# Fused attention and two MoE layers on one core: transfers weighed by issue and latency, squares of r after reload, a third staging buffer, and 42 identity matmuls among the first heads

## The chip, the cores and the metric

One NeuronCore of a Trainium2 chip runs the whole program. The metric is the device time of one execution in microseconds. The matrix engine is PE (TensorE), the others are DVE (VectorE), ACT (ScalarE), POOL (GpSimd) and SP (SyncE), which issues the DMA transfers. PE's granted clock has two levels, 1.2 and 2.4 GHz; the profile gives it as a share of the upper one.

## The reference

```python
# q, k, v: (4, 8, 576, 64); causal window of 128, ALiBi
scores = np.where(mask, q @ k.T / 8 + bias, -1e9)     # mask: 0 <= i - j < 128
x  = softmax(scores) @ v                              # heads merged: 2304 x 512
y  = (((x @ w1) * (x @ w2)) @ w3) @ w_out             # 512 -> 1024 -> 1024 -> 512
h  = np.maximum(y @ w_in, 0.0)                        # 512 -> 2048
out = (h * h) @ w_out2                                # 2048 -> 512
```

All of it is float32 (`moe_w1`, `moe_w2`, `moe_w3`, `moe_w_out`, `moe2_w_in`, `moe2_w_out` stand here as w1, w2, w3, w_out, w_in, w_out2).

## The kernel before, in words

**Arithmetic.** Most products are made from two rounded words per operand, a high and a low one, in three matmuls: high x high, high x low, low x high (`mm3`, L165 to 168). So each operand is prepared by a cast to the high word and a subtraction that gives the low word; the cast may run on ACT (`act_copy`, L171) or DVE (L221), the subtraction on DVE or POOL (L174). Native float32 matmuls take two passes of PE each instead.

**Stages.** Four follow each other, and overlap through the planner's order.
- *Heads.* 32 heads: scores of K and Q (L463 to 466), softmax on DVE, ACT and POOL, transposes by identity (L486 to 498), and probabilities times V. The heads in the set NQ have native scores, those in NV native PV (L520, L542, L543); the others use split words (L525 to 529, L549). Beside the heads, w3 @ w_out is folded into one matrix, w34, with native matmuls (L730), up to 126 us.
- *ab and y*, 126 to 526 us, among the remaining heads: x @ w1, x @ w2 and y = (a*b) @ w34, in groups of 12 matmuls of 288 columns that accumulate in a PSUM tile with the tag g. The pool ps_g has three banks of it (L156). DVE, as it takes the product out of PSUM, makes `gf` (L783), then `gt`'s words. y goes to DRAM (`y_scr`).
- *r*, 526 to 710: relu(y @ w_in) squared, with Strassen-Winograd: seven products P1 to P7 for each of 3 blocks j of 768 tokens and 8 blocks m of weights. The sums of products (L1089) are made on DVE into C; ACT does relu (L1115) and square (L1116) in place, and C is stored to DRAM (`s_scr`).
- *out*, 713 to 893: the squares times w_out2, 9 blocks t of 256 tokens, again seven products (X<-u,st and X<-u,ww, 128x256). `add_o` loads four blocks of s_scr (tags fo and fq, 128x1024), forms the sums (L1160), casts and subtracts them into operand words (tags st for t = 0 and ww).

**Words of w_in and w_out2.** They come as raw pairs of words (`w2io`), are merged by DVE and ACT (`m_load` L902, scale L215 or L294, L304, `m_last` L913) and stored to DRAM as `m_scr` (`m_store`, L919): the *merges*, 385 to 485 us. Later `add_words2` loads them back into a staging buffer, makes the Strassen combinations, and splits these into the tags u and v6. y is loaded back for j = 0, 1, 2 by `add_yops` into yA and yB. The staging buffers are st (two) and s0 (one); s0 holds the words of i0, i1 and o7.

**Order.** The order of instructions comes from `Plan` (L27): every piece of work is a task with a rank, a cost per engine it may run on, the tasks that it depends on, and the buffers that it takes and gives back. `run` keeps a model time per engine (pe, a, d, p, dma), puts the task that could start earliest next (within LOOK, the lowest rank), and picks the engine by its end plus `bias`. A result on another engine counts as ready a latency later (L253). All tasks are emitted in that order, and each engine runs its own in that order: a wait of one instruction holds all behind it on its engine. `w_dma` (L243) is the model cost of a transfer on SP's queue. `p_warm` (L616) is four 128x256 matmuls of `bm` ahead of all other work of PE.

```python
# L156 and L616
    ps_g = ps1.enter_context(tc.tile_pool(name="ps_g", bufs=3, space=PSUM))
    def p_warm():
        t = ps_t.tile([128, 512], F32, tag="t", name="t")
        for _ in range(4):
            nc.tensor.matmul(t[:, 0:256], ident, bm, start=True, stop=True)
```

Of the kernel before, what the change touches and what calls it, by code (L numbers as in the profile page):

```python
# [8 lines left out]
F32 = mybir.dt.float32  # L9
# [7 lines left out]
NV = frozenset(range(7))  # L17
RANK = dict(w34=6.25, h0=-10.7, w12=37.2, w12s=7.96, w12l=9.7)
# [9 lines left out]
class Plan:  # L28
# [9 lines left out]
    bias = dict(d=3.0, D=0.34, a=0.3, p=0.0)  # L38
# [14 lines left out]
    def run(self):  # L53
# [71 lines left out]
def fused_kernel(  # L125
# [117 lines left out]
    def w_dma(kb):  # L243
        return 0.1 + kb / 300.0
# [8 lines left out]
        dict(pe=0.25, a=0.2, d=0.12, p=0.2, dma=2.0, gate=0.0),  # L253
# [362 lines left out]
    def p_warm():  # L616
        t = ps_t.tile([128, 512], F32, tag="t", name="t")
        for _ in range(4):
            nc.tensor.matmul(t[:, 0:256], ident, bm, start=True, stop=True)

    hold("warm", "t", 1)
    add("warm", -100.0, {"pe": 5.0}, lambda e: p_warm(), [], ["warm"], ["warm"])
# [4 lines left out]
    def add_head(n, rank):  # L627
# [12 lines left out]
        if nq:  # L640
            add(f"ldq{n}", r, {"dma": w_dma(295)}, lambda e: t_load_qk(n), [f"ldq{n - 1}"] if n else [], H_("qk"))
            add(f"kn{n}", r, w_ts(576, "Dap"), lambda e: t_kn(n, e), N("ldq"))
            qd = N("kn")
        else:
            hold(f"qkraw{n}", "qkraw", 4)
            add(f"ldq{n}", r, {"dma": w_dma(590)}, lambda e: t_load_qk(n), [f"ldq{n - 1}"] if n else [], [f"qkraw{n}"])
# [6 lines left out]
        if nv:  # L653
            add(f"ldv{n}", r + 0.1, {"dma": w_dma(147)}, lambda e: t_load_v(n), N("ldq"), H_("vs"))
            vd = N("ldv")
        else:
            hold(f"vraw{n}", f"vraw{n % 2}", 2)
            add(f"ldv{n}", r + 0.1, {"dma": w_dma(147)}, lambda e: t_load_v(n), N("ldq"), [f"vraw{n}"])
# [291 lines left out]
    def add_words2(k, m, rank, stag, dep=()):  # L950
# [12 lines left out]
        for part, w, tag in (("a", 1024, "u"), ("b", 768, "u" if m < 2 else "v6")):  # L963
            hold(f"w{part}{z}", tag, n * (4 if part == "a" else 3))

# [11 lines left out]
            add(f"wh{part}{z}", rank + 0.1, w_copy(w), hi, d, [f"w{part}{z}"], g_)  # L977
# [16 lines left out]
    def add_yops(j, rank, deps):  # L994
        where = ["yA"] * 14 if j != 1 else ["yB"] * 6 + ["yA"] * 8
        for c in range(2):
            z = f"{j}{c}"
            tag, t2 = ("u", "t2a") if j == 0 else ("st", ("t2a", "t2b")[c])
# [6 lines left out]
                deps + [f"sy{b}{hf}{c + 2 * k}" for b, hf in ys_ for k in range(2)], ["ym" + z])  # L1005
# [17 lines left out]
            for pos, P in enumerate(PO):  # L1023
# [12 lines left out]
                add(f"yo0{j}{P}{c}", rank + pos, w_copy(TN), hi, [get[1] + z], [f"yo{j}{P}{c}"], g_)  # L1036
# [30 lines left out]
    def add_group(g, n, order, prod, fin, rank):  # L1067
# [17 lines left out]
        add("c1" + z, -20, w_copy(n, True), lambda e: copy(e, t_("c1", "c1"), bank[g, 1]), ["P1" + z], ["c1" + z], [f"X1{z}"])  # L1085
# [16 lines left out]
    def add_r(j, m, rank, last):  # L1102
# [8 lines left out]
        def fin(z):  # L1111
            def sq(e, c):
                x = cs[g, c]
                if e == "a":
                    nc.scalar.activation(out=x, in_=x, func=ACTF.Relu)  # L1115
                    nc.scalar.activation(out=x, in_=x, func=ACTF.Square)  # L1116
                else:
                    ENG[e].scalar_tensor_tensor(out=x, in0=x, scalar=0.0, in1=x, op0=ALU.max, op1=ALU.mult)
# [5 lines left out]
            for c in ("11", "12", "21", "22"):  # L1124
                add(f"sq{c}{z}", rank + 16, {"a": 2 * w_copy(TN)["a"]}, lambda e, c=c: sq(e, c), [f"c{c}{z}"])
# [10 lines left out]
    def add_o(t, rank, last):  # L1136
        j, t0 = divmod(256 * t, 2 * TN)
        ft = {k: ("fo" if t == 0 and k[0] == "A" else v) for k, v in FT.items()}
        for k, n in (("A11", 4), ("A12", 3), ("A21", 4), ("A22", 3), ("S1", 3), ("S2", 5)):
            hold(f"f{k}{t}", ft[k], n)  # L1140
        for k in ("A11", "A21", "A22", "A12"):
# [8 lines left out]
            col = (t0 + 128 * i) // TN  # L1150
            add(f"lf{k}{t}", rank - 20, {"dma": w_dma(524)}, ld,
# [23 lines left out]
        for pos, P in enumerate(order):  # L1175
# [63 lines left out]
    add("q2", 0, {"gate": 0.0}, lambda e: open_q2(), last_r + [f"wlao{NM - 1}", f"wlbo{NM - 1}"])  # L1239
# [18 lines left out]
    add_yops(2, 2000 + 112 - 14, done(1))  # L1258
# [62 lines left out]
```

## Time and profile before

| | us |
|---|---|
| median of 3 runs | 900.42 (900.16 to 902.66) |
| the profiled execution | 901.4 |
| its span | 899.6 |
| PE busy in the span | 871.2 |
| DVE, ACT, POOL busy | 696.4, 502.4, 205.6 |
| mean granted clock of PE | 0.992 of full |

The span goes from the first to the last instruction; the execution's own time has a little around it. A row of a timeline gives the start, how long it was from there to the end, the engine, the line, the operation with what it writes and reads, the tile, the count of instructions that it stands for, and in brackets the idle time of the engine before it with what ended it. Matmuls are pipelined: the distance from one start to the next is what each costs, and the duration of one is longer. A line of waits gives the total, the number and the longest.

### The profile page before, as it was taken

The page shows a single profiled execution, that of the slowest core. Times are in us where ns is not written, and L with a number is a line of the kernel's source. Part 1 is how long each engine was busy: PE and PEld are TensorE (multiplying, and loading weights), DVE is VectorE, ACT ScalarE, POOL GpSimd, SP SyncE. Part 2 cuts the span into 40 slices and gives each one's busy share as a digit, 9 for nine tenths or more (in the row PEclk, how much of TensorE's full clock was granted, in tenths as well). Part 3 has the DMA queues.
Part 4 walks back from the last instruction along what each step waited for, and adds up shares of the span by engine and source line. Part 5 has one row for each costly group of instructions (what it writes and reads, how often), then busy time and mean ns, then how long its engine had stood idle before and what let it go on. Part 6 is the DMA issues. An engine that isn't in the chain of part 4 may idle for free.

```text
span 899.6 us, 16224 instructions
## 1 busy us (share of the span) xinstructions
PE 871.2 (97%) x5888; PEld 805.3 (90%) x5888; DVE 696.4 (77%) x1402; ACT 502.4 (56%) x1086; POOL 205.6 (23%) x252
## 2 busy tenths in 40 slices
PE   7999999999999899999999999989999799999998
PEld 4544479999999899999989999989999799999998
DVE  5777888788877888878666938776568888998882
ACT  5777775656566567676323336776677733222220
POOL 4423422213231232311000134542136400000000
PEclk8999999999999999999999999999999899999999
DMA  7786312433426425163667034643385475445310
GB/s 239 270 296 201 127 48 80 133 74 81 134 49 186 114 72 157 35 186 101 233 233 237 25 109 153 204 165 116 113 255 176 144 210 165 118 136 152 101 54 30
DMA packets 90704, 128.43 MB, mean 143 GB/s; under 512 B 8832, under 2 KB 70784, under 8 KB 88576
## 3 DMA queue, kind: packets, MB, share of 16 engines
q1 hardware_dynamic: 90624, 127.40, 45.6%
q8 instruction: 46, 0.75, 0.3%
q14 instruction: 34, 0.28, 0.1%
HBM read 90.67 MB, written 36.70 MB: 142 GB/s over the span
## 4 chain that ended last, share of the span: by engine, by line
PE 80%; DMA 9%; DVE 7%; ACT 2%; issue 2%; SPq 1%; POOL 0%; DVEq 0%; ACTq 0%; POOLq 0%
PE X L168 13%; PE X L167 13%; PE X L166 13%; PE g L166 7%; PE g L168 7%; PE g L167 7%; PE g L730 7%; DMA u<-in_w2io_dram 3%; DMA m_scro<-u 2%; PE s L463 2%; PE a L520 2%; PE s L466 1%; PE t L486 1%; PE s L465 1%; DMA m_scri<-u 1%
## 5 line engine op out<-in xcount | busy, mean ns | idle before, releaser
L166 PE MATMUL g<-x,wu 128*128 128x288 f32 x512 | 154.2, 301 | 3.1 <-DVE gf L783 2.0
L168 PE MATMUL g<-x,wu 128*128 128x288 f32 x512 | 151.1, 295 | 1.7 <-DVE wu L174 1.7
L167 PE MATMUL g<-x,wu 128*128 128x288 f32 x512 | 151.6, 296 | 0.1
L166 PEld LDWEIGHTS g<-x,wu 128*128 128x128 f32 x512 | 96.3, 188 | 4.9 <-DVE gf L783 3.7
L168 PEld LDWEIGHTS g<-x,wu 128*128 128x128 f32 x512 | 96.5, 188 | 1.9 <-DVE wu L174 1.9
L167 PEld LDWEIGHTS g<-x,wu 128*128 128x128 f32 x512 | 96.8, 189 | 0.3 <-DVE x L174 0.3
L166 PE MATMUL g<-gt,wu 128*128 128x288 f32 x256 | 76.6, 299 | 0.2 <-DVE gt L221 0.2
L167 PE MATMUL g<-gt,wu 128*128 128x288 f32 x256 | 75.8, 296 | 0.1
L168 PE MATMUL g<-gt,wu 128*128 128x288 f32 x256 | 75.5, 295 | 0.0
L1089 DVE TENSOR_TENSOR C<-X,U 128x384 f32<-128x384 f32 (+1 forms) x99 | 51.0, 518 | 24.4 <-PE X L168 11.1
L443 ACT ACTIVATE e<-e,st 128x256 f32<-128x256 f32 (+1 forms) x128 | 60.5, 475 | 14.0 <-DVE st L435 13.6
L1115 ACT ACTIVATE C<-C 128x384 f32<-128x384 f32 x96 | 49.5, 515 | 32.6 <-DVE C L1089 32.5
L168 PE MATMUL X<-yA,u 128*128 128x384 f32 x192 | 65.2, 340 | 1.6 <-DVE u L174 1.6
L167 PE MATMUL X<-yA,u 128*128 128x384 f32 x192 | 65.0, 339 | 0.0
L166 PE MATMUL X<-yA,u 128*128 128x384 f32 x192 | 65.0, 339 | 0.0
L938 POOL TENSOR_TENSOR st<-st 128x256 f32<-128x256 f32 (+1 forms) x52 | 46.7, 916 | 76.4 <-DMA st<-m_scri 37.1
L730 PE MATMUL g<-raw 128*128 128x512 f32 x128 | 63.2, 625 | 0.0
L213 POOL TENSOR_SCALAR e<-e,st 128x256 f32<-128x256 f32 (+1 forms) x61 | 31.0, 520 | 122.1 <-DVE st L453 73.0
L167 PE MATMUL X<-u,ww 128*128 128x256 f32 x198 | 55.4, 280 | 0.0
L168 PE MATMUL X<-u,ww 128*128 128x256 f32 x198 | 55.4, 280 | 0.0
L166 PE MATMUL X<-u,ww 128*128 128x256 f32 x198 | 55.4, 280 | 0.0
L171 ACT ACTIVATE pt<-t 128x512 fp32r<-128x512 f32 (+1 forms) x64 | 38.2, 597 | 28.0 <-PE t L498 18.5
(218 smaller groups left out, 2651.4 us busy)
## 6 DMA issues: line engine op xcount, KB each, us to landing
s_scr<-C SPq DMA_DIRECT2D x96, 192.0 KB, 1.9
u<-in_w2io_dram SPq DMA_DIRECT2D x32, 512.0 KB, 4.4
qkraw<-in_qk_dram SPq DMA_DIRECT2D x46, 288.0 KB, 4.3
fo<-s_scr SPq DMA_DIRECT2D x20, 512.0 KB, 4.5
raw<-in_w3t_dram SPq DMA_DIRECT2D x8, 1024.0 KB, 6.1
raw<-in_w_dram SPq DMA_DIRECT2D x8, 1024.0 KB, 5.1
fq<-s_scr SPq DMA_DIRECT2D x16, 512.0 KB, 4.6
y_scr<-ye SPq DMA_DIRECT2D x32, 144.0 KB, 3.1
```

What stands on the lines that cost most here:

```text
L166: nc.tensor.matmul(o, wh, xh, start=start, stop=False)
L167: nc.tensor.matmul(o, wh, xl, start=False, stop=False)
L168: nc.tensor.matmul(o, wl, xh, start=False, stop=stop)
L171: nc.scalar.activation(out=o, in_=i, func=ACTF.Copy)
L213: nc.gpsimd.tensor_scalar(out=o, in0=i, scalar1=c, scalar2=1.0, op0=ALU.mult, op1=ALU.mult)
L443: nc.scalar.activation(out=e, in_=e, func=ACTF.Exp, bias=st[:, 0, i:i + 1], scale=-1.0, accum_out=st[:, 1, i:i + 1],)
L463: nc.tensor.matmul(o, qb, d["kh"][:, k0:k1], start=True, stop=True)
L520: nc.tensor.matmul(a[:, 128 * kb:128 * kb + w], vs[:, kb, :], pt[:, 0, c:c + w], start=kb == 0, stop=kb == 2,)
L730: nc.tensor.matmul(gw[fi], wl, wr, start=c == 0, stop=c == 7)
L938: ENG[e].tensor_tensor(out=o, in0=a, in1=b, op=op)
L1089: nc.vector.tensor_tensor(out=t_(o, tag), in0=bank[g, P], in1=cs[g, i], op=ALU.add)
L1115: nc.scalar.activation(out=x, in_=x, func=ACTF.Relu)
```

## The change

1. *Model of transfers.* `w_dma` counts 0.55 us per DMA issue, or kb/300 if that is more, in place of 0.1 + kb/300; a transfer's latency is 3.0, was 2.0. Some ranks and DVE's bias are other numbers. The model only sets the order: with these numbers the merges begin earlier, and the last DVE sequences in which a merge is locked between groups' evacuations are three, where before they were about five.
2. *Fills.* `p_warm` goes. 42 matmuls of the identity with itself (128x128, native) are tasks of very high rank that the planner places where PE would otherwise be idle for over 0.15 us of model time. All of them write one tile of the tag g, which is given back after the last.
3. *NV* holds nine heads, not seven.
4. *Squares.* In r, `fin` only takes the relu; the square is made on ACT after the reload in `add_o` (tasks fs, 128x1024), and what used the loaded block now uses its square.
5. *Third staging buffer.* s0 also takes the words of i2, o2 and o5 and the first half of y for j = 1 and 2, whose load for j = 1 waits only for the third words of i and no longer for the eighth; o7 goes to st.
6. *High words* of the weights, of y for j > 0, of out's operands, and the copy c1 are cast on ACT alone (`w_act`), no longer on DVE.
7. *Border.* The last group of r takes its products in the order 1, 7, 2, 4, 6, 5, 3; the operands of P1 and P2 of t = 0 have a rank lower by 30; the pool q2 opens after the words of o5, not o7.

PE's matmuls go from 5742 to 5770, DVE's instructions from 1404 to 1383, ACT's from 928 to 895, POOL's from 257 to 239; SP issues 426 in both.

```diff
-NV = frozenset(range(7))
-RANK = dict(w34=6.25, h0=-10.7, w12=37.2, w12s=7.96, w12l=9.7)
+FILL = 9000
+NFILL = 42
+NV = frozenset(range(9))
+RANK = dict(w34=5.49, h0=-13.66, w12=35.93, w12s=7.96, w12l=7.68)
-    bias = dict(d=3.0, D=0.34, a=0.3, p=0.0)
+    bias = dict(d=2.02, D=0.34, a=0.3, p=0.0)
-                t0 = 0.0
+                t0 = free.get("pe", 0.0) + 0.15 if rank >= FILL else 0.0
+    def w_act(n):
+        return {"a": 0.2 + n * 0.00094}
-    def w_dma(kb):
-        return 0.1 + kb / 300.0
+    def w_dma(kb, n=1):
+        return max(0.55 * n, kb / 300.0)
-        dict(pe=0.25, a=0.2, d=0.12, p=0.2, dma=2.0, gate=0.0),
+        dict(pe=0.25, a=0.2, d=0.12, p=0.2, dma=3.0, gate=0.0),
-    hold("warm", "t", 1)
-    add("warm", -100.0, {"pe": 5.0}, lambda e: p_warm(), [], ["warm"], ["warm"])
+    fills = [None]
+
+    def p_fill(i):
+        if i == 0:
+            fills[0] = ps_g.tile([128, 512], F32, tag="g", name="g")
+        nc.tensor.matmul(fills[0][:, 0:128], ident, ident, start=True, stop=True)
+
+    NF = NFILL
+    hold("fill", "g", NF)
+    for i in range(NF):
+        add(f"fill{i}", FILL + i, {"pe": 0.22}, lambda e, i=i: p_fill(i), [f"fill{i - 1}"] if i else [],
+            [] if i else ["fill"], ["fill"])
...
-            add(f"wh{part}{z}", rank + 0.1, w_copy(w), hi, d, [f"w{part}{z}"], g_)
+            add(f"wh{part}{z}", rank + 0.1, w_act(w), hi, d + room, [f"w{part}{z}"], g_)
-            tag, t2 = ("u", "t2a") if j == 0 else ("st", ("t2a", "t2b")[c])
+            tag, t2 = ("u", "t2a") if j == 0 else (("s0", "st")[c], ("t2a", "t2b")[c])
...
                 if e == "a":
                     nc.scalar.activation(out=x, in_=x, func=ACTF.Relu)
-                    nc.scalar.activation(out=x, in_=x, func=ACTF.Square)
...
-        add_group(g, TN, PO, prod, fin, rank)
+        add_group(g, TN, (1, 7, 2, 4, 6, 5, 3) if last else PO, prod, fin, rank)
...
+            def square(e, k=k):
+                x = fa[t, k]
+                if e == "a":
+                    nc.scalar.activation(out=x, in_=x, func=ACTF.Square)
...
+            add(f"fs{k}{t}", rank - 1, w_act(1024), square, [f"lf{k}{t}"], [], [f"f{k}{t}"])
...
+            early = -30 if t == 0 and P in (1, 2) else 0
...
-    add("q2", 0, {"gate": 0.0}, lambda e: open_q2(), last_r + [f"wlao{NM - 1}", f"wlbo{NM - 1}"])
+    add("q2", 0, {"gate": 0.0}, lambda e: open_q2(), last_r + ["wlao5", "wlbo5"])
...
-        add_words2("i", m, 1040 + m if m < 2 else 2000 + 7 * m - 12, "s0" if m < 2 else "st", prev if m < 2 else ["ph", *prev])
+        add_words2("i", m, 1040 + m if m < 3 else 2000 + 7 * m - 12, "s0" if m < 3 else "st", prev if m < 3 else ["ph", *prev])
...
-    add_yops(1, 2000 + 56 - 14, ["wlai7", "wlbi7"])
+    add_yops(1, 2000 + 56 - 14, (["wlai2", "wlbi2", "ph"], ["wlai7", "wlbi7"]))
...
-        add_words2("o", m, 2090 + 7 * m, "st" if m < NM - 1 else "s0", prev)
+        add_words2("o", m, 2090 + 7 * m, "s0" if m in (2, 5) else "st", prev)
```

How it moves instructions, at three places. **PE's first rows**, with the scores s of the first heads, the transposes t and, after the change, the fills g<-ident. Before:

```order
L619 MATMUL t<-bm,ident 128x256 x4
L463 MATMUL s<-kn,qn 128x192
L463 MATMUL s<-kn,qn 128x256 x3
L463 MATMUL s<-kn,qn 128x192 x2
L463 MATMUL s<-kn,qn 128x256 x3
L486 MATMUL t<-ident,e 128x128 x4
L463 MATMUL s<-kn,qn 128x192
L494 MATMUL t<-swap,p_132 128x128
```

After:

```order
L628 MATMUL g<-ident 128x128 x12
L469 MATMUL s<-kn,qn 128x192
L469 MATMUL s<-kn,qn 128x256 x3
L628 MATMUL g<-ident 128x128
L469 MATMUL s<-kn,qn 128x192
L628 MATMUL g<-ident 128x128 x2
L469 MATMUL s<-kn,qn 128x192
L469 MATMUL s<-kn,qn 128x256 x3
L628 MATMUL g<-ident 128x128 x3
L469 MATMUL s<-kn,qn 128x192
L492 MATMUL t<-ident,e 128x128 x4
L628 MATMUL g<-ident 128x128 x4
```

The four warm-up matmuls are gone, twelve fills stand first, and single fills stand between the scores and the transposes of the first heads. Thirty stand before the end of head 2's transposes, nine more among the next heads, two in r's j = 1, and one behind r.

**PE where r ends and out begins**, after the change, with the buffers' numbers (X<-yA,v6 is the last product of r, X<-u,st the first of out):

```order
L170 MATMUL X_8254<-yA_7561,v6_6716 128x384
L171 MATMUL X_8254<-yA_7561,v6_6716 128x384
L628 MATMUL g_144<-ident_107 128x128
L169 MATMUL X_8285<-u_7730,st_8231 128x256
L170 MATMUL X_8285<-u_7730,st_8231 128x256
L171 MATMUL X_8285<-u_7730,st_8231 128x256
```

The last fill stands here, and g_144 is the tile that the first fill took: one of the three g banks is kept from the program's start until this row.

**DVE at the same border** (C: sums of r; u and v6: low words of w_out2; fq: sums of the loaded blocks f; st and ww: low words of out's operands). Before:

```order
L1089 TENSOR_TENSOR C_8338<-X_8326,U3_8293 128x384
L174 TENSOR_TENSOR u_8306<-st_8193,u_8306 128x1024
L174 TENSOR_TENSOR v6_8308<-st_8193,v6_8308 128x768
L174 TENSOR_TENSOR u_8345<-s0_8235,u_8345 128x1024
L174 TENSOR_TENSOR v6_8349<-s0_8235,v6_8349 128x768
L174 TENSOR_TENSOR st_8352<-fo_7627,st_8352 128x1024
L1160 TENSOR_TENSOR fq_8364<-fo_7795,fo_7823 128x1024
L1160 TENSOR_TENSOR fq_8393<-fq_8364,fo_7627 128x1024
```

After:

```order
L1102 TENSOR_TENSOR C_8273<-X_8254,U4_8264 128x384
L1102 TENSOR_TENSOR C_8278<-X_8200,U4_8264 128x384
L177 TENSOR_TENSOR u_8240<-st_8101,u_8240 128x1024
L177 TENSOR_TENSOR v6_8275<-st_8101,v6_8275 128x768
L1180 TENSOR_TENSOR fq_8314<-fo_7754,fo_7780 128x1024
L1180 TENSOR_TENSOR fq_8317<-fq_8314,fo_7576 128x1024
L177 TENSOR_TENSOR st_8312<-fo_7601,st_8312 128x1024
L177 TENSOR_TENSOR ww_8281<-fo_7780,ww_8281 128x1024
```

Before, the low word of the first operand, st, stood behind two pairs of u and v6. After, it has left this row and is made on POOL; what stands behind one pair u and v6 is the two sums fq and then the next operand's low word.

## Rows read from the trace of the kernel before

**Rows 1.** The page's part 1: busy us (share of the span) xinstructions.

```profile
PE 871.2 (97%) x5888; PEld 805.3 (90%) x5888; DVE 696.4 (77%) x1402; ACT 502.4 (56%) x1086; POOL 205.6 (23%) x252
```

**Rows 2.** Busy time by stage; columns are start:end, length, PE, PEld, DVE, ACT, POOL.

```profile
30.00:126.00 96.00, 96.00 (x322) 48.18 (x323) 77.55 (x156) 71.80 (x150) 30.85 (x34) 1.00 0.59 196
...
440.00:505.00 65.00, 61.93 (x451) 59.84 (x451) 44.49 (x74) 22.40 (x43) 4.76 (x4) 1.00 0.57 194
...
705.00:725.00 20.00, 14.66 (x88) 14.13 (x87) 17.10 (x21) 13.73 (x21) 3.75 (x5) 0.83 0.41 130
725.00:893.00 168.00, 168.00 (x1426) 168.00 (x1425) 140.31 (x169) 44.53 (x48) 0.00 (x0) 1.00 0.42 119
```

**Rows 3.** Timeline of PE, 3 to 31 us: start, duration, engine, line, operation.

```profile
3.37 3.78 PE L619 MATMUL t<-bm,ident 128*128 128x256 f32 x8 [3.37 <-POOL bm L204]
...
25.37 0.27 PE L495 MATMUL t<-ident,p 128*128 128x128 f32 x1
25.48 0.27 PE L496 MATMUL t<-ident,e 128*128 128x128 f32 x1
...
27.71 1.94 PE L520 MATMUL a<-pt,vn 128*64 128x512 f32 x6
...
30.16 0.65 PE L486 MATMUL t<-ident,e 128*128 128x128 f32 x4
```

**Rows 4.** Busy time by window around the first heads, with the granted clock (PEclk).

```profile
14.00:20.00 6.00, 4.78 (x13) 2.73 (x14) 5.80 (x9) 5.06 (x12) 2.17 (x2) 0.55 0.93 340
20.00:22.00 2.00, 2.00 (x7) 0.89 (x5) 1.26 (x8) 0.40 (x1) 1.59 (x5) 0.66 0.02 6
```

**Rows 5.** Timeline of POOL, the identity matrix.

```profile
1.11 0.30 POOL masks.py:199 TENSOR_SCALAR_AFFINE_SELECT ident<-ident 128x128 f32<-128x128 f32 x1
```

**Rows 6.** Timeline of PE, a head with split p and v.

```profile
103.71 0.81 PE L525 MATMUL a<-pt,vs 128*128 128x512 f32 x1
104.37 0.28 PE L526 MATMUL a<-pt,vs 128*128 128x256 f32 x1
...
105.38 1.10 PE L730 MATMUL g<-raw 128*128 128x512 f32 x2
```

**Rows 7.** Waits of DVE, 440 to 505: us in total, times, longest.

```profile
DVE u L215 <- DMA u<-in_w2io_dram: 16.0, 6, 4.9
```

**Rows 8.** Timeline of DVE in the last merges.

```profile
454.42 0.70 DVE L215 TENSOR_SCALAR u<-u 128x1024 f32<-128x1024 f32 x1 [3.32 <-DMA u<-in_w2io_dram]
455.03 0.45 DVE L783 TENSOR_TENSOR gf<-g,a_sb 128x288 f32<-128x288 f32 x1
```

**Rows 9.** Timeline of PE beside them.

```profile
455.54 0.40 PE L166 MATMUL g<-x,wu 128*128 128x288 f32 x1 [1.14 <-DVE gf L783]
```

**Rows 10.** Waits of PE in the r stage, 526.5 to 705.

```profile
PE X L167 <- DVE yB L174: 2.3, 3, 1.0
PE X L168 <- DVE u L174: 1.6, 2, 1.3
```

**Rows 11.** Timeline of PE at the border of r and out.

```profile
709.53 0.34 PE L168 MATMUL X<-yA,u 128*128 128x384 f32 x1
713.25 0.38 PE L166 MATMUL X<-u,st 128*128 128x256 f32 x1 [3.38 <-ACT st L171]
...
715.71 0.58 PE L168 MATMUL X<-u,st 128*128 128x256 f32 x1 [1.96 <-DVE st L174]
...
721.00 0.34 PE L168 MATMUL X<-u,st 128*128 128x256 f32 x1
```

**Rows 12.** Timeline of DVE at the border of r and out.

```profile
709.96 0.56 DVE L1089 TENSOR_TENSOR C<-X,U 128x384 f32<-128x384 f32 x1 [0.51 <-PE X L168]
710.44 1.21 DVE L174 TENSOR_TENSOR u<-st,u 128x1024 fp32r<-128x1024 f32 x1
711.57 0.95 DVE L174 TENSOR_TENSOR v<-st,v 128x768 fp32r<-128x768 f32 x1
```

**Rows 13.** The page's part 5: the squares on ACT in r.

```profile
L1115 ACT ACTIVATE C<-C 128x384 f32<-128x384 f32 x96 | 49.5, 515 | 32.6 <-DVE C L1089 32.5
```

More of the change, by code (lines that the diff above doesn't have):

```diff
@@ L613, in t_xl @@
         sub(ENG[e], t[:, 1], HD[b * H + 2 * p]["xf"][:, hf * HALF:(hf + 1) * HALF], f(t[:, 0]))
[L616 to L619, printed above, removed]
-    hold("warm", "t", 1)
-    add("warm", -100.0, {"pe": 5.0}, lambda e: p_warm(), [], ["warm"], ["warm"])
+    fills = [None]
[8 more added lines that the diff above has]
+            [] if i else ["fill"], ["fill"])
     add("ptz1", 0.0, {"p": 0.5}, lambda e: new_pt(True))
@@ L640, in add_head @@
         if nq:
[L641 removed]
+            add(f"ldq{n}", r, {"dma": w_dma(295, 2)}, lambda e: t_load_qk(n), [f"ldq{n - 1}"] if n else [], H_("qk"))
             add(f"kn{n}", r, w_ts(576, "Dap"), lambda e: t_kn(n, e), N("ldq"))
@@ L645, in add_head @@
             hold(f"qkraw{n}", "qkraw", 4)
-            add(f"ldq{n}", r, {"dma": w_dma(590)}, lambda e: t_load_qk(n), [f"ldq{n - 1}"] if n else [], [f"qkraw{n}"])
+            add(f"ldq{n}", r, {"dma": w_dma(590, 2)}, lambda e: t_load_qk(n), [f"ldq{n - 1}"] if n else [], [f"qkraw{n}"])
             R = [f"qkraw{n}"]
@@ L653, in add_head @@
         if nv:
-            add(f"ldv{n}", r + 0.1, {"dma": w_dma(147)}, lambda e: t_load_v(n), N("ldq"), H_("vs"))
+            add(f"ldv{n}", r + 0.1, {"dma": w_dma(147, 2)}, lambda e: t_load_v(n), N("ldq"), H_("vs"))
             vd = N("ldv")
@@ L964, in add_words2 @@
             hold(f"w{part}{z}", tag, n * (4 if part == "a" else 3))
+            room = ["ph"] if k == "i" and tag == "v6" else []
             def hi(e, part=part, w=w, tag=tag):
@@ L1004, in add_yops @@
             add("yl" + z, rank - 3, {"dma": w_dma(786)}, lambda e, c=c, tag=tag: y_load(j, c, tag),
-                deps + [f"sy{b}{hf}{c + 2 * k}" for b, hf in ys_ for k in range(2)], ["ym" + z])
+                deps[c] + [f"sy{b}{hf}{c + 2 * k}" for b, hf in ys_ for k in range(2)], ["ym" + z])
             def S_(i, c=c, t2=t2):
@@ L1083, in t_ @@
             return x
-        add("c1" + z, -20, w_copy(n, True), lambda e: copy(e, t_("c1", "c1"), bank[g, 1]), ["P1" + z], ["c1" + z], [f"X1{z}"])
+        add("c1" + z, -20, w_act(n), lambda e: copy(e, t_("c1", "c1"), bank[g, 1]), ["P1" + z], ["c1" + z], [f"X1{z}"])
         def plus(nm, o, tag, P, i, deps, ho, gives):
@@ L1138, in add_o @@
         ft = {k: ("fo" if t == 0 and k[0] == "A" else v) for k, v in FT.items()}
-        for k, n in (("A11", 4), ("A12", 3), ("A21", 4), ("A22", 3), ("S1", 3), ("S2", 5)):
+        for k, n in (("A11", 5), ("A12", 4), ("A21", 5), ("A22", 4), ("S1", 3), ("S2", 5)):
             hold(f"f{k}{t}", ft[k], n)
@@ L1186, in lo @@
                 sub(ENG[e], x[:, 1], fa[t, k].rearrange("p c t -> p (c t)"), f(x[:, 0]))
-            add(f"oh{P}{t}", rank + pos, w_copy(1024), hi, [src[P]] + ([] if tag == "st" else ["q2"]) + (["wlao6", "wlbo6"] if t == 0 and tag == "st" else [])
+            early = -30 if t == 0 and P in (1, 2) else 0
+            add(f"oh{P}{t}", rank + pos + early, w_act(1024), hi, [src[P]] + ([] if tag == "st" else ["q2"]) + (["wlao6", "wlbo6"] if t == 0 and tag == "st" else [])
                 + chain[P], [f"ow{P}{t}"], F(k))
-            add(f"ol{P}{t}", rank + pos, w_tt(1024), lo, [f"oh{P}{t}"], [], F(k))
+            add(f"ol{P}{t}", rank + pos + early, w_tt(1024), lo, [f"oh{P}{t}"], [], F(k))
         g = ("o", t)
```

28 lines of the change are left out of this document (15 added, 13 removed).

## Prediction, before the changed kernel was run

> **What bounds the kernel now.** The page's engine line comes first: PE is busy in 871.2 of 899.6 us [rows 1], so a gain can only be one of two things, PE time that is idle or PE time at the lower clock. The busy times by stage say where that time is [rows 2]. From 30 to 126 us, and again from 725 to 893, PE is full at a granted clock of 1.00: there every matmul that is added or taken away counts whole. From 440 to 505 it idles 65 - 61.93 = 3.07 us at full clock; around the border of the r and the out stage (705 to 725) it idles 5.34 us and the clock averages 0.83. The start has its own rows: PE's first matmul begins at 3.37 [rows 3], and in 14 to 22 the granted clock is 0.55 and 0.66 [rows 4], between the levels of 1.2 and 2.4 GHz. DVE is the second engine: 140.31 of 168 us in the out stage.
>
> **The start (fills for the warm-up).** Out go four 128x256 matmuls, 3.78 us at 3.37, which waited for bm [rows 3]. In come 42 identity matmuls on one bank; the first twelve need ident alone, which is ready at 1.11 + 0.30 = 1.41 [rows 5]. Thirty stand before the end of head 2's transposes, in places where the planner sees PE idle. Price: identity products stand 25.48 - 25.37 = 0.11 apart in one pass [rows 3]; a fill is two passes, 0.22, at full clock, and 42 are 9.2 us. What can be won is the half-clock loss: 4.78 busy x 0.45 + 2.00 x 0.34 = 2.83 us [rows 4]. PE also starts some 1.9 us earlier (3.37 against about 1.5), but nine fills stand later, in a stretch where PE is full anyway [rows 2], 9 x 0.22 = 2.0 us on the path; these two cancel. I take **-2.8**. Below, the early start is kept as well and the late fills fall in gaps: -4.7. Above, the clock falls as before and half of the fills (4.6) lie on the path with 2.8 of them in old gaps: +1.8.
>
> **Two more heads with native PV.** A native head takes from 27.71 to 30.16, 2.45 us [rows 3]; a split one 105.38 - 104.37 = 1.01 and its first matmul, at most 103.71 to 104.37 [rows 6]; that gives 1.0 to 1.7, and I take 1.25, since that first matmul starts in the shadow of the one before. Two heads are 2 x 1.2 = **+2.4**, in a stretch where PE is full, so on the path. Ends: +1.5 and +2.8. What DVE and ACT save by not splitting p and v there is worth nothing, as PE waits for neither in that stretch.
>
> **Merges, and the bank that the fills hold.** From 446 to 485 each w2io merge waits on DVE for its load: 16.0 us in six waits [rows 7]. Evacuations of g stand behind them: the load is late by 3.32, then scale, then gf at 455.03 [rows 8], and PE waits 1.14 for that gf [rows 9]. With the new DMA costs the merges start earlier, and the order leaves three such cycles where five were: 2/5 of 3.07, a gain of 1.2. Against it, the fills' tile is one of three g banks and is kept until the last fill behind r, so that ab and y work with two banks. With three, PE runs two groups of 12 matmuls ahead of a late evacuation, with two only one, 12 x 61.93/451 = 1.6 us. I charge one group once, as the cycles left stand together: +1.6. Net +0.4, which with the idle in other places of that stretch I call **0**. Ends: all of the idle goes, -3.1; or every DMA wait of DVE reaches PE, 16.0 - 3.1 = +12.9.
>
> What the rows show of such idle moments is that the granted clock stays 1.00 between 440 and 505 [rows 2]. The Trainium skill (TensorE: Matmul & The Clock Gate, section "A second HAM failure mode: psum-queue depth-cycling") says that PE idling briefly between groups, while it cycles through PSUM banks, makes the clock go back and forth. By that rule two banks would be worse than the idle time alone, and the sum would be a rival's, below; this trace speaks against it.
>
> **Third staging buffer and the r stage.** In r, PE waited 2.3 us in three waits for yB's lo halves on DVE, and 1.6 in two for u's [rows 10]. Before, y's hi casts for j = 1 stood on DVE among the subtractions; now they go to ACT, and the first half of y is loaded into the third buffer as soon as w2i's third words are split, not its eighth. I take the 2.3 as gone, half of 1.6 as gone with it (0.7), and add two fills that stand in r's j = 1, +0.4: **-2.6**. Below: all of it and no price for the fills, -3.9. Above: a cast on ACT arrives later than DVE's did, one wait of the longest kind that the rows show, +1.0.
>
> **The border of r and out.** The last r matmul ends at 709.87, out starts at 713.25, stops until 715.71 and runs its next 24 matmuls at half clock until 721.00 [rows 11]. At full clock the 26 matmuls take 26 x 168.00/1426 = 3.06 us [rows 2], so 11.13 - 3.06 = 8.07 are lost, some 2.5 of them to the clock. After the change the operand of product 1 is made early (its subtraction moves to POOL), and product 1, 24 matmuls and 2.8 us, can run at once. Product 2's lo half is the next that is late. DVE has ahead of it two C sums, u, v and two sums of f: 2 x 0.56 + 1.21 + 0.95 + 2 x 1.21, and then its own 1.21, all by [rows 12]: 6.9 us after the last r matmul. So PE idles 6.9 - 3.1 = 3.8, and if the clock falls again, another 2.5: 3.8 to 6.3 lost, a gain of 4.3 to 1.8. The one fill planned there covers 0.22. I take **-2.0**, near the end with the fallen clock, for it fell here after idle times of 3.38 and 1.96. Above: the early operand comes late, +1.0.
>
> **Squares and casts moved.** In r, ACT loses 96 squares of 0.515 us [rows 13], half of what it does behind a C sum, and C's way to the store gets shorter by as much. In out it gains 36 squares of 128x1024, at most 0.515 x 1024/384 = 1.4 us each, 49 us beside 44.53 of 168 [rows 2]. Each stands between a load and a Strassen sum. The loads of block t+1 run while block t multiplies (168/9 = 18.7 us), which hides it: **0**. Without that cover it is one square per block, 9 x 1.4 = +12. SP issues as many DMAs as before. The casts that leave DVE for ACT ease DVE, which PE does not wait for outside the places named.
>
> **Sum**: -2.8 + 2.4 + 0 - 2.6 - 2.0 = -5.0. The profiled execution took 901.4, its span 899.6 and 1.8 around it, so 896.4; the median of the runs is 1.0 lower, 900.4, hence **895.4**.
>
> **Rivals.**
> 1. *Slower: the held bank.* From the point where an evacuation is late by more than one group, 1.6 us, two banks leave PE waiting for gf. For it: DVE stands still up to 4.9 us at a time [rows 7], and with three banks a wait of 3.32 already reached PE with 1.14 [rows 8, 9]. Against it: the merges now start earlier. Price +12.9 in the place of 0: 908.3. A longer wait of the squares (+12) would look like it in out. Chance 0.12. The Trainium skill (Perfetto Trace Analysis, section "Optimizing Tensor Performance") has independent matmul groups rotate through PSUM banks, so that an evacuation lies beside the next group; that speaks for this rival, and the trace agrees as far as three banks go.
> 2. *Slower: the clock falls in the gaps of the two-bank stretch*, the page's rule as a mechanism of this kernel. Each of three remaining cycles would cost what the clock cost at the border, 2.5: +7.5, 902.9, more with the waits themselves. Against it is the 1.00 of [rows 2]. Chance 0.03.
> 3. *No change: the gaps move.* The planner's new DMA costs reorder all queues; the r gaps and the border idle come back elsewhere at their old size, and only start and heads are left: -2.8 + 2.4, 900.0. It is also what comes out if the fills don't hold the clock and half of the other gains stay. Chance 0.22.
> 4. *Better: the lower ends.* -4.7 + 1.5 - 3.1 - 3.9 - 4.3 = -14.5: 886. It needs all the parts to go well; half of that, 891, is likelier. Chance 0.18.
>
> **How the numbers follow.** The forecast has 0.45. The range goes from the fourth case's end, 886, to 906: it takes in the forecast, the third and the second, part of a smaller form of the first, and leaves out its full price; that is under 2 in 10. What a measurement of this kernel can tell is 0.3%, 897.7 to 903.1. Faster: 0.43 of the forecast and the fourth case, 0.61. Same: 0.02 and most of the third, 0.21. Slower: the first two and 0.03 of the third, 0.18.
>
> **What would show each step.** Granted clock 1.00 from 12 to 24 and head 2 finished about 3 us earlier: the fills work; a clock of 0.5 to 0.7 there refutes it. PV heads 7 and 8 with the native rows' 2.45. Waits of PE on gf between 400 and 505: about 2 in sum says two banks are enough, over 8 the first rival. No wait on yB in r. Product 1 of out right behind r, then one gap of some 4 us before product 2; a gap under 2 would mean DVE's queue was shorter than I think. Waits of PE in out behind an ACT square would make the last part wrong. The forecast is wrong if out or the g stage shows new PE idle of over 3 us.

## The result, and the profile after

The changed kernel takes **888.25 us** in the median of four runs (885.33 to 889.08); on the same chip the kernel before takes 901.15. The ratio is **0.985, with a 95% interval of 0.9822 to 0.9877**. The forecast was 895.4, a gain of 5.0; the direction is right, the gain is over twice as large, 12.9.

PE's line of the page answers to [rows 1]. The span went from 899.6 to 886.3:

```profile
PE 873.9 (99%) x5964; PEld 812.9 (92%) x5964; DVE 683.0 (77%) x1381; ACT 515.1 (58%) x1053; POOL 191.9 (22%) x234
```

PE is busy 2.7 us longer, in a span that is 13.3 shorter: its idle time fell from 28.4 to 12.4 us. Busy time by stage (start:end, length, PE, PEld, DVE, ACT, POOL, then the granted clock) answers to [rows 2]:

```profile
440.00:500.00 60.00, 58.54 (x435) 57.56 (x434) 45.61 (x87) 19.99 (x38) 1.02 (x1) 1.00 0.43 151
...
520.00:600.00 80.00, 80.00 (x459) 80.00 (x458) 58.23 (x97) 42.49 (x83) 43.38 (x38) 1.00 0.50 173
...
690.00:710.00 20.00, 16.66 (x101) 16.25 (x100) 17.03 (x21) 13.55 (x20) 3.39 (x3) 0.92 0.50 153
...
730.00:880.00 150.00, 150.00 (x1273) 150.00 (x1272) 114.30 (x134) 77.31 (x81) 0.00 (x0) 1.00 0.37 109
```

r, which starts at 520.8, has no idle left; the end of r and the first of out lie in 690 to 710, with 3.34 us idle and a clock of 0.92, against 5.34 and 0.83. What PE waited for, in the whole execution (total, times, longest), the larger rows of the kernel before:

```profile
PE X L166 <- ACT st L171: 3.4, 1, 3.4
PE t L619 <- POOL bm L204: 3.4, 1, 3.4
PE t L486 <- POOL e L213: 2.7, 3, 1.2
PE X L167 <- DVE yB L174: 2.3, 3, 1.0
PE g L166 <- DVE gf L783: 2.0, 4, 1.1
PE X L168 <- DVE st L174: 2.0, 1, 2.0
PE g L168 <- DVE wu L174: 1.7, 1, 1.7
```

and of the changed kernel:

```profile
PE X L171 <- DVE st L177: 2.1, 1, 2.1
PE g L169 <- DVE gf L795: 1.8, 3, 1.2
PE t L500 <- DVE pt L177: 1.5, 2, 1.2
PE g L628 <- POOL ident masks.py:199: 1.5, 1, 1.5
PE X L169 <- ACT st L174: 1.2, 1, 1.2
```

The waits on POOL's e rows, on wu, on yB are gone. Those on gf [rows 9] went from 2.0 to 1.8, and the border has two waits as before [rows 11].

Four points in PE's timeline cut the execution: the first g<-x matmul, the last matmul into g, the last into X of r, the last of out. The lengths between them, all from the profiled executions (the totals are medians), for the kernels of this text:

| | what it is | total | up to ab | ab and y | r | out |
|---|---|---|---|---|---|---|
| before | | 900.4 | 126.6 | 399.7 | 183.1 | 186.8 |
| changed | | 888.3 | 129.9 | 390.7 | 178.2 | 184.1 |
| e1 | before + transfer model | 914.8 | 126.8 | 408.8 | 183.4 | 191.7 |
| e2 | before + NV, ranks, bias | 897.8 | 127.7 | 393.1 | 181.0 | 187.0 |
| e3 | before + fills | 897.6 | 127.4 | 393.3 | 185.1 | 186.3 |
| e4 | changed, bank given back early | 885.2 | 129.2 | 388.3 | 177.9 | 184.3 |
| e5 | changed, one fill | 885.6 | 129.1 | 388.4 | 177.9 | 185.1 |
| e6 | changed, staging as before | 896.1 | 128.5 | 391.2 | 182.4 | 188.2 |
| e7 | changed, squares at the store | 892.5 | 129.1 | 390.4 | 181.5 | 186.2 |
| e8 | changed, old NV, ranks, bias | 906.0 | 123.1 | 417.4 | 177.9 | 184.0 |
| e9 | changed, old bias | 888.3 | 129.3 | 391.1 | 178.2 | 184.3 |
| e10 | changed, NV = 7 | 896.0 | 125.9 | 401.9 | 177.9 | 185.4 |
| e11 | changed, latency 2.0 | 889.7 | 127.7 | 395.2 | 181.7 | 182.1 |
| e12 | changed, planned without fills | 890.7 | 124.3 | 398.9 | 177.9 | 184.3 |
| e13, e14 | ranks moved, NV = 9 / 7 | 886.1 / 901.1 | 128.3 / 124.2 | 390.3 / 410.0 | 177.9 / 177.9 | 184.3 / 183.9 |
| e15, e16 | others moved, NV = 9 / 7 | 884.7 / 888.0 | 128.7 / 125.0 | 388.3 / 397.5 | 177.9 / 177.9 | 184.3 / 183.9 |
| e17 | changed, old ranks, NV = 9 | 897.0 | 129.2 | 399.7 | 177.9 | 185.1 |
| e18 | before, NV = 9 | 896.9 | 129.8 | 391.2 | 183.1 | 187.0 |

Behind the last matmul both kernels take 3.3 us. So the forecast's terms and the measured ones are: up to ab -0.4, measured **+3.3**; ab and y 0, measured **-9.0**; r -2.6, measured **-4.9**; out -2.0, measured **-2.7**; sum -5.0 against -13.3 in the two profiles.

### The profile page after: what moved, and what is told of

Its sections match the earlier page's. It is cut to its first block, busy times and chain, and to the rows that moved or that the text cites. A ratio compares the mean times of both kernels' runs of the same rounds, so it can differ in the third digit from the quotient of the medians.

```text
span 886.3 us, 16329 instructions
## 1 busy us (share of the span) xinstructions
PE 873.9 (99%) x5964; PEld 812.9 (92%) x5964; DVE 683.0 (77%) x1381; ACT 515.1 (58%) x1053; POOL 191.9 (22%) x234
## 4 chain that ended last, share of the span: by engine, by line
PE 89%; DVE 6%; DMA 3%; issue 1%; POOL 0%; SPq 0%; ACT 0%; DVEq 0%; POOLq 0%
PE X L171 13%; PE X L169 13%; PE X L170 13%; PE g L169 9%; PE g L170 9%; PE g L171 9%; PE g L742 7%; PE s L469 2%; DMA u<-in_w2io_dram 2%; PE a L526 2%; PE s L472 1%; PE s L471 1%; PE t L492 1%; DMA m_scro<-u 1%; PE a L535 1%
## 5 line engine op out<-in xcount | busy, mean ns | idle before, releaser
L174 ACT ACTIVATE a_sb<-g 128x288 f32<-128x288 f32 x64 | 26.2, 409 | 60.0 <-PE g L171 58.6
L174 ACT ACTIVATE ww<-fq 128x1024 fp32r<-128x1024 f32 x35 | 37.0, 1059 | 40.4 <-PE X L171 22.4
```

What stands on the lines that cost most here:

```text
L174: nc.scalar.activation(out=o, in_=i, func=ACTF.Copy)
```

## The experiments

**Parts of the change in the kernel before (e1 to e3), and the bank (e4).** e1 takes the new `w_dma` and latency, e2 `NV`, `RANK` and `bias`, e3 the block of fills in place of `p_warm`.

> The kernel before with part 1 of the change alone: a transfer counts 0.55 us per issue or kb/300, latency 3.0. The stage of ab and y (first g<-x matmul to last g matmul) took 399.8 us before and 390.7 after the change; PE idle in it goes with 13.3 us of lost time before and 4.7 after. Theory T1 (the model of transfers is what takes the waits out of ab and y): this kernel's ab/y stage is 391 to 394 us and the total about 892 to 895. Theory T2 (the bias of DVE, ranks and NV do it): 398 to 401, total 899 to 902. Theory T3 (any new order moves such waits by a few us, without a rule): anything between 394 and 406.

> The kernel before with NV = 9 heads, the new ranks and DVE's bias of 2.02 alone. T2 (less work planned for POOL, whose late e rows made PE wait 2.7 us, and two heads without splits): ab/y stage 391 to 395 us; the start up to the first g<-x matmul gets 2.4 us longer (126.6 to 129). T1: ab/y stays at 398 to 401, total 902 to 904. T3: anything between 394 and 406.

> The kernel before with the 42 fills in place of the warm-up, all else old. My prediction's start term: the first g<-x matmul comes 0 to 3 us earlier than 126.6, granted clock 1.00 from 14 to 22 us. What the changed kernel suggests instead: only about 1 us is won by head 2 and the later fills give it back, so 126 to 128. The bank that the fills hold: if two banks of g cost time, ab/y is 402 or longer; if they cost none, 396 to 401.

The transfer model alone makes the kernel before slower, ratio 1.0177 (1.015 to 1.0203): ab and y are 9.1 us longer, out 4.9. T1 is refuted for that kernel. NV, ranks and bias alone shorten ab and y by 6.6, as T2 said, yet the total only to 0.9979 (0.9961 to 0.9998). The fills alone bring 0.9971 (0.995 to 0.9992), with ab and y 6.4 shorter although one bank is held: a new order by itself moves such lengths by several us, as T3 has it. Up to ab the fills win nothing here: the first g<-x comes at 127.4, before at 126.6. r is 2.0 longer, but not by its waits. The r stage of the kernel before, and behind it that of e3:

```profile
526.40:709.50 183.10, 179.24 (x1010) 177.46 (x1009) 133.09 (x223) 129.80 (x256) 78.25 (x78) 1.00 0.51 169
```

```profile
520.60:705.80 185.20, 181.71 (x1011) 180.06 (x1009) 132.73 (x223) 130.23 (x256) 79.05 (x78) 0.98 0.51 168
```

PE's idle time is 3.9 before and 3.5 in e3; the clock averages 0.98 in e3's r, where it was 1.00. What made it fall there isn't shown.

```diff
-        nc.tensor.matmul(fills[0][:, 0:128], ident, ident, start=True, stop=True)
+        if i < 39:
+            nc.tensor.matmul(fills[0][:, 0:128], ident, ident, start=True, stop=True)
```

> The changed kernel in its own order, but the last three fills (two in r, one behind it) are not emitted, so that the tile of the fills is given back behind the 39th, before ab begins, and ab and y rotate three banks. Bank theory (two banks make evacuations late): the waits of PE on gf, 1.8 us, fall to under 0.5 and the time falls by 1.5 to 2 us. Rival (the waits that are left are DVE's order and the merges' transfers, not banks): the gf waits stay, and only the fills in r are won, 0.4 us: within 1 us of the changed kernel.

885.15 (885.08 to 886.66). The waits of PE in ab and y, in the changed kernel (129.9 to 520.6), the first row:

```profile
PE g L169 <- DVE gf L795: 1.8, 3, 1.2
```

and in e4 (129.2 to 517.6), all there are:

```profile
PE t L500 <- DVE pt L177: 1.5, 2, 1.1
```

The waits on gf are gone, and the stage took 388.3 in place of 390.7. e5, which holds no bank either, took 388.4, and e9, whose instructions are the changed kernel's row for row and which is a repeat of it, 391.1. So the held bank costs 2.3 to 2.8 us of the stage. The totals agree, though they come from several chips: of the eight runs of the changed kernel and e9 one took 885.33 and the others 887.84 or more, while all eight of e4 and e5 took 886.66 or less.

**No fills (e5), staging (e6), squares (e7), old ranks (e8)**, all in the changed kernel. e5 emits only fill 0:

```diff
+        if i == 0:
+            nc.tensor.matmul(fills[0][:, 0:128], ident, ident, start=True, stop=True)
```

> The changed kernel in its own order with only the first of the 42 fills emitted: no warm-up, and the bank is free. Theory F (the fills hold PE's clock up while the first heads wait): the granted clock in 10 to 30 us falls to between 0.5 and 0.8, and the first g<-x matmul comes at 129.2 (as with 39 fills) less the nine late fills, 2.0, plus the clock's loss of 2.5 to 3.5: 129.5 to 130.7; total as with the bank free, 885.2, plus 0.5 to 1.5. Rival (the first heads are bound by the softmax chain, and fills there only fill): the clock falls but the start ends at 127 to 128 and the total is 883 to 884.

885.55 us, as with 39 fills. PE's timeline at the end of head 2's PV, in the kernel before:

```profile
37.25 0.33 PE L543 MATMUL b<-pt,vn 64*64 64x64 f32 x2
```

with the fills, in the changed kernel:

```profile
1.46 5.49 PE L628 MATMUL g<-ident 128*128 128x128 f32 x24 [1.46 <-POOL ident masks.py:199]
...
22.09 0.27 PE L504 MATMUL t<-ident,e 128*128 128x128 f32 x1
...
23.11 0.56 PE L469 MATMUL s<-kn,qn 64*128 64x192 f32 x2 [0.53 <-DVE st L441]
...
24.02 1.94 PE L526 MATMUL a<-pt,vn 128*64 128x512 f32 x6
...
36.84 0.32 PE L549 MATMUL b<-pt,vn 64*64 64x64 f32 x2
```

and without, in e5:

```profile
4.80 4.20 PE L469 MATMUL s<-kn,qn 64*128 64x192 f32 x10 [2.54 <-DVE kn L218]
...
16.02 0.42 PE L501 MATMUL t<-ident,p 128*128 128x128 f32 x1
16.23 0.42 PE L502 MATMUL t<-ident,e 128*128 128x128 f32 x1
...
23.24 0.27 PE L504 MATMUL t<-ident,e 128*128 128x128 f32 x1
...
23.96 1.94 PE L526 MATMUL a<-pt,vn 128*64 128x512 f32 x6
...
36.78 0.32 PE L549 MATMUL b<-pt,vn 64*64 64x64 f32 x2
```

Without fills PE runs at half clock until about 18.8 us (the transposes at 16 us stand 0.21 apart, against 0.11 in [rows 3]; the trace's first record of the granted clock, 1.00, stands at 18.83) and idles 2.54 before the first scores, but head 2's last PV matmul comes at 36.78, not later than 36.84 (36.20 in e4, with 39 fills). Neither theory held whole: the clock is low at first, as F says, and it costs nothing up to ab. The rows show where the lead goes: at the last transpose of head 1 the changed kernel is 1.15 us ahead (22.09 against 23.24), then it waits 0.53 for a softmax row of DVE and does four more fill passes, two on each side of that wait, and head 1's PV starts at 24.02, in e5 at 23.96. In e4 that wait is absent and head 2 is 0.6 ahead of e5, but by ab this is gone too. The fills also cost little but their bank: ab starts at 129.1 without, at 129.2 with them (e4).

> The changed kernel with the staging of before: s0 for i0, i1 and o7 alone, y for j = 1 and 2 from st, both halves after the eighth words of i. My prediction's term: the r stage, 178.2 us with the change and 183.1 before, has its waits on yB again (2.3 us) and half of the others, so 180.5 to 181.5, and the total is 2.5 us longer, 890 to 891. Rival (the waits on yB went because the hi casts left DVE, not by the buffer): r stays at 178 to 179. The ab/y stage should stay at 390 to 392 in either case.

```diff
-            tag, t2 = ("u", "t2a") if j == 0 else (("s0", "st")[c], ("t2a", "t2b")[c])
+            tag, t2 = ("u", "t2a") if j == 0 else ("st", ("t2a", "t2b")[c])
...
-        add_words2("o", m, 2090 + 7 * m, "s0" if m in (2, 5) else "st", prev)
+        add_words2("o", m, 2090 + 7 * m, "st" if m < NM - 1 else "s0", prev)
...
```

896.09 us: r is 4.2 us longer and out 4.1. Its waits from r to the border:

```profile
PE X L169 <- ACT st L174: 6.2, 1, 6.2
PE X L170 <- DVE yB L177: 2.3, 1, 2.3
PE X L170 <- DVE yA L177: 1.2, 1, 1.2
```

The buffer is worth more than I gave it, in both places: y's halves arrive early enough in r, and the words of w_out2 are split in time, so that the operand of product 1 (st) no longer stands 6.2 us behind r.

> The changed kernel with the squares where they were, on ACT behind the relu in r, 96 of 128x384, none in out. My prediction costs this part at nothing: total 887 to 889.5, r 178 to 179, out 184 to 185. Rival (with ACT as the only engine for the high words, the 49 us of squares in r would make ACT late there): r 179.5 to 182 with PE waits on yB, yA or u behind ACT, total 890 to 892.

```diff
+                nc.scalar.activation(out=x, in_=x, func=ACTF.Relu)
+                nc.scalar.activation(out=x, in_=x, func=ACTF.Square)
...
-            add(f"fs{k}{t}", rank - 1, w_act(1024), square, [f"lf{k}{t}"], [], [f"f{k}{t}"])
...
```

892.46 us (390.4 in ab and y, r 3.3 longer, out 2.1). The new wait in r:

```profile
PE X L169 <- DVE C L1102: 2.1, 2, 1.6
```

PE waits for DVE's C sums. What these waited for in e7's r, 519 to 701:

```profile
DVE C L1102 <- DMA s_scr<-C: 16.8, 12, 2.8
DVE C L1102 <- ACT C L1128: 6.2, 7, 3.1
```

and in the changed kernel's, 520 to 699:

```profile
DVE C L1102 <- DMA s_scr<-C: 2.2, 3, 1.3
```

So with the square in r DVE's next sums wait for the stores that give the buffers C back (16.8 us in place of 2.2) and for ACT (6.2). The squares were not free in r.

> The changed kernel with NV = 7, the old ranks and the old bias of DVE, all the rest new. On the kernel before, these numbers took ab/y from 399.7 to 393.1 us, and the transfer model alone took it to 408.8. If they are what takes the waits out of ab/y (T2): ab/y here is 397 to 402, total 895 to 900. If it is the order as a whole, without one part that does it (T3): ab/y 392 to 400 with other waits than those of before. If neither is needed: 390 to 391.5, and the start is 2.4 shorter, total 886.

906 us, ratio 1.0074 (1.0045 to 1.0103), ab and y 26.7 us longer. With the old NV, ranks and bias the rest of the change is slower than the kernel before.

**Which of those numbers (e9 to e12).** One line each: `bias` d back to 3.0; `NV` back to 7; `dma=2.0`; the fills' block left out.

> The changed kernel with DVE's bias at 3.0 as before, NV and the ranks new. With all three old the stage of ab and y took 417.4 us, with all three new 390.7. If the bias does it (with 3.0 the planner gives head work to POOL, whose rows PE then waits for): ab/y 405 to 417, with waits of PE on POOL e of 2 us or more, total 900 to 912. If it is the ranks or NV: ab/y 389 to 394, total 887 to 891.

> The changed kernel with seven heads with native PV, as before, bias and ranks new. My prediction: two native heads cost 2.4 us of PE at the start and give nothing back, so the first g<-x matmul comes at 127.5 (129.9 with nine), ab/y stays at 390 to 391.5 and the total is 886. Rival (splitting p and v of two more heads loads DVE and POOL ahead of ab, and makes the heads late): the start is as much shorter, but ab/y is 393 to 400 and the total 888 to 896.

> The changed kernel with a transfer's latency of 2.0 in the planner's model, as before, the cost per issue new. The transfer model alone made the kernel before 15 us slower. If it earns something in the changed kernel (the rows of issue to landing show 3.1 to 6.1 us for the kernel before, so 3.0 is nearer): ab/y and r each get 1 to 4 us longer, waits on words that come by DMA appear, total 890 to 896. If it is only another order: 885 to 893 without more waits on DMA.

> The changed kernel without fills and without a warm-up in the plan, so that the planner knows of three banks of g. Leaving the fills out at the changed order gave 885.5. If a plan for three banks is better still: ab/y 386 to 388.4, total 882 to 885. If any new plan only moves waits (T3): ab/y 388 to 397, total 885 to 894.

The bias does nothing with the new ranks and nine heads: the order comes out the same. Seven native heads cost 7.7 us in the total: ab starts 4.0 earlier and the stage is 11.2 longer. With a latency of 2.0 it is 889.72 (4.5 more in ab and y and 3.5 in r, less in the other stages), without a wait on DMA that PE shows; its ratio, 0.9885 (0.9857 to 0.9913), can't be told from the changed kernel's. Planning without fills gives 890.65, 5 us more than leaving the fills out at the fixed order, though the plan knows of a bank more: T3 again.

**Heads or order (e13 to e18).** Since any input of the planner moved ab and y, two small moves of ranks were run, each with nine and seven native heads, and nine heads alone in two other plans.

> The changed kernel with two ranks moved by a little (w34 5.49 to 5.6, w12 35.93 to 36.1), nine native heads: the same work in another order. End of the g stage (last g matmul): 520.6 us in the changed kernel. T3 (the order as such moves the waits): 520 to 530, and it says how far a change of nothing but two small numbers goes. If nine native heads carry the gain: 519 to 523.

> The same small move of two ranks with seven native heads. Theory N (two heads fewer to split take work off DVE and POOL ahead of the stage that they limit; with seven it ended 7.3 us later, at 527.9): the end of the g stage is 4 us or more later than with nine and the same ranks. T3: the pair differs by anything between -5 and +8.

> The changed kernel with two other ranks moved (h0 -13.66 to -13.3, w12l 7.68 to 7.9), nine native heads. As for the first small move: 519 to 523 if the nine heads carry the gain, up to 530 if the order as such does.

> The second small move with seven native heads. Theory N: the g stage ends 4 us or more later than with nine and the same ranks. T3: between -5 and +8.

> The changed kernel with the old ranks and nine native heads; with the old ranks and seven the g stage ended at 540.5 us, total 906. Theory N: nine heads alone bring it to 521 to 530. If the ranks do it: 535 to 541.

> The kernel before with nine native heads, nothing else; its g stage ended at 526.4 us, and with nine heads and the new ranks at 520.8. Theory N: 519 to 523. If the ranks do it, the two heads cost their 2.4 us: 527 to 530. T3: anything between 519 and 533.

Four pairs differ in NV alone, and a fifth, e17 and e8, in NV and DVE's bias. In all five the g stage ends earlier with nine heads (the sum of two columns of the table), and PE is idle for less time in ab and y (the stage's length less PE's busy time in it):

| pair, nine and seven heads | end of the g stage | PE idle in ab and y |
|---|---|---|
| e18 and before | 521.0, 526.3 | 4.4, 9.5 |
| changed and e10 | 520.6, 527.8 | 3.6, 10.1 |
| e13 and e14 | 518.6, 534.2 | 2.9, 14.7 |
| e15 and e16 | 517.0, 522.5 | 1.6, 7.2 |
| e17 and e8 | 528.9, 540.5 | 8.9, 18.0 |

That is 5.3 to 15.6 us for the same step, 9.0 in the mean. Each end is from one profiled execution. The medians of the totals differ the same way, by 2.2 to 15.0. For e18 (ratio 0.9974, 0.9944 to 1.0004) and for e15 and e16 the intervals do not separate the two. With nine heads and small moves of ranks the end is 517.0 to 520.6, so in the changed plan such moves hardly matter; the old ranks still cost 8.3 with nine heads.

In the kernel before, what nine heads take away is seen on DVE. Its low words pt with seven heads (count, shortest, median, longest in ns, first and last start):

```profile
L174 DVE TENSOR_TENSOR pt<-t,pt x50: 672/690/692, 97.4 to 425.9; 128x512 fp32r<-128x512 f32 x50
```

and with nine heads in e18:

```profile
L174 DVE TENSOR_TENSOR pt<-t,pt x46: 672/691/694, 134.6 to 409.8; 128x512 fp32r<-128x512 f32 x46
```

Four are gone, 2.8 us; of v's words, two casts and two subtractions fewer are made, on DVE and POOL together. From 126 to 526, in the kernel before:

```profile
126.00:526.00 400.00, 390.46 (x2967) 384.24 (x2967) 313.03 (x785) 227.39 (x573) 84.78 (x112) 1.00 0.41 122
```

and in e18:

```profile
126.00:526.00 400.00, 395.62 (x3004) 390.05 (x3003) 305.35 (x783) 229.54 (x577) 87.61 (x111) 1.00 0.42 123
```

DVE has 7.7 us less to do in the same stretch, and PE 5.2 us more, as e18's r begins inside it. In the changed plan the saved work is not on DVE. ab and y of the changed kernel, and behind it of e10, seven heads:

```profile
129.90:520.60 390.70, 387.14 (x2962) 383.52 (x2961) 309.57 (x774) 226.01 (x563) 75.61 (x106) 1.00 0.41 125
```

```profile
125.90:527.70 401.80, 391.67 (x2970) 386.14 (x2969) 308.62 (x775) 234.65 (x587) 92.46 (x112) 1.00 0.42 122
```

With seven, POOL has 16.9 us more to do and ACT 8.6, DVE 1.0 less: the planner gives the heads' rows to other engines. In the pair that is furthest apart the waits are on the heads' softmax. e14, seven heads, 124 to 534:

```profile
PE t L492 <- POOL e L216: 5.2, 2, 3.5
PE s L471 <- DVE st L441: 4.7, 2, 3.3
```

and its PE from 200 to 300, behind it that of e13, nine heads:

```profile
200.00:300.00 100.00, 93.03 (x683) 90.94 (x682) 81.45 (x221) 66.42 (x171) 28.43 (x34) 0.95 0.52 154
```

```profile
200.00:300.00 100.00, 100.00 (x778) 99.62 (x778) 82.24 (x227) 71.43 (x177) 20.86 (x30) 1.00 0.45 131
```

With seven, PE is idle 7 us here and some of the rest is at the lower level (0.95); with nine it is full at 1.00.

## Why the prediction was right or wrong, point by point

- **Two native heads: this step failed.** The text said that the work saved on DVE and ACT "is worth nothing, as PE waits for neither in that stretch". It looked at the stretch where the heads stand, 30 to 126, and gave the stage behind it 0; that stage measured -9.0. The saved work is paid back there, where late rows of DVE, POOL and ACT are what PE waits for: nine heads take 5 to 12 us of PE's idle time out of ab and y in the five pairs. The price was about right: in the changed kernel a native head takes 2.44 (104.93 to 107.37), as forecast. Up to ab the pair before and e18 differs by +3.2, where I had +2.4; 1.2 of that is lost by the end of head 2 (38.45, before 37.25), where e18's clock stayed low for longer (0.50 from 20 to 22 us, against 0.66). The other pairs have +3.7 to +6.1. The gain in ab and y is 8.5 in that pair, and I had 0. The sum is -5.3 where I had +2.4.
- **Merges and the bank: right in kind, wrong in what was counted.** I counted only the idle of 440 to 505, 3.1 us. The idle from 126 to 440 was larger (6.5 us, most of it on e, wu and st), and the sum holds nothing for it but "other places" at 0. The held bank costs 2.3 to 2.8, where I charged 1.6; the rival that would have made it 12.9 didn't come. The Trainium skill (Perfetto Trace Analysis, section "Optimizing Tensor Performance") asks for groups to rotate through PSUM banks; the runs agree, by those 2.3 us. What the Trainium skill (TensorE: Matmul & The Clock Gate, section "A second HAM failure mode: psum-queue depth-cycling") reports of the clock doesn't show: with two banks the clock from 440 to 500 is 1.00.
- **The start: mechanism there, gain not.** The lower clock of [rows 4] is gone, but head 2 ends 0.4 us earlier (1.1 in e4), not 2.8. The step that failed is that PE's lost clock was on the path: e5 has it again and ends head 2 as early. The nine late fills, which I charged with 2.0, cost 0.7 at most: e4 is 0.6 ahead of e5 at head 2 and 0.1 behind at ab.
- **r: under-sized.** The yB waits went, as forecast; r gained 4.9 in place of 2.6. Every gap went, not those alone on which I counted. A gap also costs more than its listed idle: five gaps with 3.9 us of idle [rows 10] were worth 5.2 (183.1 to 177.9 in e4, which has no fills in r). A matmul of 0.34 that follows another starts 0.18 after it and not after its end, which adds five times 0.16; the last 0.5 stays open. And the price of 0 for the squares was wrong: e7 loses 3.3 in r and 2.1 in out without that part.
- **The border: right in the wait, with two gaps for one.** Forecast: product 1 at once, then PE waits until DVE has made product 2's low half, 6.9 us behind the last matmul of r. PE's timeline:

```profile
698.81 0.34 PE L171 MATMUL X<-yA,v 128*128 128x384 f32 x1
698.98 0.39 PE L628 MATMUL g<-ident 128*128 128x128 f32 x2
699.12 0.36 PE L169 MATMUL X<-u,st 128*128 128x256 f32 x1
...
703.44 0.39 PE L169 MATMUL X<-u,st 128*128 128x256 f32 x1 [1.21 <-ACT st L174]
...
706.08 0.39 PE L171 MATMUL X<-u,st 128*128 128x256 f32 x1 [2.14 <-DVE st L177]
```

DVE's, behind u and v:

```profile
702.41 1.22 DVE L1180 TENSOR_TENSOR fq<-fo 128x1024 f32<-128x1024 f32 x1
703.66 1.23 DVE L1180 TENSOR_TENSOR fq<-fq,fo 128x1024 f32<-128x1024 f32 x1
704.81 1.22 DVE L177 TENSOR_TENSOR st<-fo,st 128x1024 fp32r<-128x1024 f32 x1
```

  r ends at 699.15 and the low half at 704.81 + 1.22 = 706.03, 6.9 later; PE goes on at 706.08. The idle time came as two gaps, 1.21 for product 2's high word on ACT and 2.14 for the low one, 3.35 in sum where I had 3.8. The gain is 2.7 with what follows (forecast 2.0). But e6 shows that the early operand came from the third buffer, which I had counted for r alone.
- **The transfer model** was costed only through the merges. By itself it makes the kernel before 15 us slower (e1); no term of mine had that. What it gives in the changed kernel isn't shown: e11 undoes its latency alone, and no run undoes its cost per issue.
- **Rivals.** "Better: the lower ends" (886) came nearest, for a reason that it didn't name. The range held the time.

e15 (884.7, two runs) and e4 (885.2) have the lowest medians; beside the kernel before their ratios, 0.9835 (0.9778 to 0.9891) and 0.9848 (0.9822 to 0.9875), can't be told from the changed kernel's 0.985.

What stays open: how much of the 9.0 in ab and y is the two heads and how much the particular order. The heads give 5.3 to 15.6 in five pairs; new plans with the same heads moved the end of the g stage by 5.6 (e3 against the kernel before) and 5.7 us (e12 against e5), as much as the two smallest pairs. The casts on ACT (part 6) and the border's order (part 7) were not undone by themselves.

## What to carry to other kernels

Where an order is planned, work taken off the other engines is priced in the stage where they are late, not in the stage where the work stood. Count every gap of the bottleneck engine by who ends it before calling a stage neutral. A clock that is lost ahead of a place where the engine waits for another can cost nothing: look for who ends the chain. And a plan's numbers are judged together: the same transfer model cost 15 us in one setting and was part of the best in another, so single parts, undone or added, do not sum.

## What the runs showed that was not expected

The granted clock of a window at the very start can read 1.00 while PE is at the lower level. In e5, PE's transposes at 16.02 and 16.23 stand 0.21 apart, as at half clock, and the window's row says 1.00, although the trace has no record of the clock before 18.83:

```profile
14.00:20.00 6.00, 5.31 (x18) 2.83 (x17) 5.21 (x11) 4.53 (x12) 1.39 (x3) 1.00 1.00 302
```

So the spacing of equal matmuls was the safer reading there. The kernel before also spread more than its first three runs told: 895.4 to 904.1 over the chips, while e4, e5 and e9 stayed within 1.6 us.
